# Two subtractions of a query softmax moved from GpSimd to VectorE in a fused attention and gated-MLP kernel

## The chip, the cores and the metric

The kernel runs on one core of a Trainium2 chip. A core has a matrix engine (TensorE, "PE" in the profile, with its weight loads shown apart as "PEld"), VectorE ("DVE"), ScalarE ("ACT"), GpSimd ("POOL") and SyncE ("SP", which here only issues DMAs). Each engine runs its own list of instructions in order and waits on semaphores where it needs another engine's result. The metric is the device time of one execution in microseconds; lower is better.

## The reference

Four batches of 12480 tokens with 128 channels go through an attention that passes over 49 agent tokens, and then through a two-layer MLP whose gate is x - tanh(x):

```python
def sm(a, b):
    s = scale * (a @ b.transpose(0, 2, 1))
    s = s - s.max(-1, keepdims=True)
    e = np.exp(s)
    return e / (e.sum(-1, keepdims=True) + 1e-09)
a2k = sm(agents, k)
agent_v = a2k @ v
q2a = sm(q, agents)                 # the query softmax: 12480 x 49 per batch
x = q2a @ agent_v
h = x @ w_in                        # 128 -> 2048
g = h - np.tanh(h)
out = g @ w_out                     # 2048 -> 128
```

All inputs are float32 and so is the result.

## The kernel before

Phase 1 of a batch (`phase1`) computes the agents' softmax over the keys, multiplies it with the values, and folds the result into `w_in` (`project`): what is left of the attention output and the first MLP layer is then one matmul of the query softmax `p` (49 columns per token) with a 49 x 2048 matrix. To keep float32 accuracy with the faster float32r matmuls, operands are carried as a rounded "high" part and a "low" part, the difference. `p` is kept as 98 columns (49 high, 49 low, tile `pp`), and the folded matrix as `awh` and `awl`.

The main loop walks over 100 blocks of 500 tokens (the last of each batch has 480), 25 to a batch, and over 8 steps per block, two of the 16 chunks of 2048 in each. One step is:

- TensorE: four matmuls into a two-bank PSUM tile `h` (`m1`, L538 and L539);
- ScalarE: `y = tanh(h)` (L548) and `z = y*y` (L550);
- VectorE: `g = h * z` (L553), which is the gate up to a factor for the small `h` that occur here;
- GpSimd: `gh`, the rounded high part of `g` (`high`, L582);
- VectorE: `gl = g - gh`, the low part (`low`, L587);
- TensorE: six matmuls of `gh` and `gl` with `w_out`, summed in one PSUM tile `misc` over the block's 8 steps (`m2`, L600, L601, L602). In one step of every second block `gh` and `gl` are left out and a plain float32 matmul is used instead (L598).

`gh`, `gl`, `y`, `z` and `g` have 3, 2, 2, 2 and 4 buffers; `h` has 3 PSUM buffers and `misc` 2, which the running sum shares with every smaller product.

Beside this main stream run side jobs as Python generators: the query softmax of the next pair of blocks (`q_softmax`, started once per pair, 50 in all), the transposes of `pp` (`q_transpose`, L525), and the pieces of phase 1 of the next batch. Every step of the main loop calls `next` once on each job that is under way, so a job's pieces between two `yield`s are spread over successive steps. What is recorded that way is then ordered for each engine by a scheduler, which holds to data dependencies and a few manual ones.

The query softmax of one pair works on a tile of 126 rows x 8 groups x 49. TensorE writes the scores to a `misc` tile (L494). VectorE takes the row maximum `qm` (L502). ScalarE copies the scores to SBUF as `qe` (L503), GpSimd subtracts the maximum there (L505), ScalarE takes the exponential (L507). VectorE sums (`qs`, L509), adds epsilon (L510), takes the reciprocal (L511) and scales `qe` (L512); that last one is called MUL below. ScalarE writes the rounded high half of `pp` (L515), and GpSimd writes the low half, `qe` minus that (L517).

The first softmax is stepped by hand in `fast` with `next(q0)`, between the pieces of the first batch's phase 1 (L701 to L714).

Of the kernel before, what the change touches and what calls it, by code (L numbers as in the profile page):

```python
# [12 lines left out]
F32 = mybir.dt.float32  # L13
# [6 lines left out]
ALU = mybir.AluOpType  # L20
# [4 lines left out]
A = 49  # L25
# [6 lines left out]
TT = 126  # L32
TG = 120
GT = 8
# [63 lines left out]
class Build:  # L98
# [386 lines left out]
    def q_softmax(self, halves, qt, res, TT=TT):  # L485
        nc = self.nc
        ps = self.misc()
        for t in range(GT):
            b, at, w = halves[t // BT]
            at += min(t % BT * TT, w - TT)  # L490
            for r in range(0, TT, QUART):
                m = min(QUART, TT - r)
                to = ps[r : r + m, t * A : (t + 1) * A]
                nc.tensor.matmul(to, qt[:, at + r : at + r + m], self.ag[:, b, :], start=True, stop=True)  # L494
        yield
        yield
        pv = ps[:TT, : GT * A].rearrange("p (t a) -> p t a", a=A)
        m = self.small.tile([128, GT], F32, tag="qm", name="qm")
        e = self.small.tile([128, GT, A], F32, tag="qe", name="qe")
        ev = e[:TT]  # L500
        s = self.small.tile([128, GT], F32, tag="qs", name="qs")
        nc.vector.tensor_reduce(m[:TT], pv, axis=AX.X, op=ALU.max)  # L502
        nc.scalar.copy(ev, pv)  # L503
        yield
        nc.gpsimd.tensor_tensor(ev, ev, m[:TT, :, None].broadcast_to([TT, GT, A]), ALU.subtract)  # L505
        yield
        nc.scalar.activation(ev, ev, AF.Exp, scale=SCALE)  # L507
        yield
        nc.vector.tensor_reduce(s[:TT], ev, axis=AX.X, op=ALU.add)  # L509
        nc.vector.tensor_scalar(s[:TT], s[:TT], EPS, None, ALU.add)  # L510
        nc.vector.reciprocal(s[:TT], s[:TT])  # L511
        nc.vector.tensor_tensor(ev, ev, s[:TT, :, None].broadcast_to([TT, GT, A]), ALU.mult)  # L512
        yield
        pp = self.small.tile([128, GT, A2], F32R, tag="pp", name="pp")
        nc.scalar.copy(pp[:TT, :, :A], ev)  # L515
        yield
        nc.gpsimd.tensor_tensor(pp[:TT, :, A:], ev, pp[:TT, :, :A].bitcast(F32), ALU.subtract)  # L517
        res.append(pp)

    def q_transpose(self, pp, half, res, w, TT=TT):  # L520
# [117 lines left out]
    def fast(self):  # L638
        nc, tc = self.nc, self.tc
# [4 lines left out]
        qt, pp, pT = {}, {}, {}  # L644

        def q_src(p):
            at = column(2 * p)
            return self.qT[:, at : at + width(2 * p) + width(2 * p + 1)]
# [11 lines left out]
        with ExitStack() as first:  # L660
            self.begin(first, "first")
            p1 = self.phase1(0)
            raws = [None] * 8

            def load_raw(c):
                raws[c] = self.raw_w_in(c) if c < 4 else self.raw_w_out(c - 4)

            self.wf = self.keep.tile([128, FF], F32R, tag="awh", name="awh", bufs=2).bitcast(F32)
            loads = []
            for g in range(NG):  # L670
                if g % 2 == 0 and 0 < g < 10:
                    loads.append((load_raw, g // 2 - 1))
                loads.append((self.k0, g))
            q1_load = lambda p: qt.update({p: self.q_load(q_src(p))})
            loads.append((q1_load, 0))
            for g in range(NG):
                loads.append((self.v0, g))
            loads += [(load_raw, 4), (q1_load, 1)] + [(load_raw, c) for c in (5, 6, 7)]
            free = K0

            def load(more):
                nonlocal free
                free += more
                while loads and (free > 0 or loads[0][0] not in (self.k0, self.v0)):
                    f, g = loads.pop(0)
                    free -= f in (self.k0, self.v0)
                    f(g)

            load(0)
            for g in range(NG):  # L690
                run(p1[g])
                load(1)
                if g % 2 == 1 and 2 < g < 11:
                    self.load_w_in((g - 3) // 2, raws[(g - 3) // 2])
            at = self.count() - 1
            run(p1[NG])
            run(p1[NG + 1])
            q0 = q_job(0)
            av = p1[NG + 3 : 2 * NG + 3]
            for g in range(NG):  # L700
                if g == Q0:  # L701
                    next(q0)
                    next(q0)
                    next(q0)
                next(av[g])
                next(av[g])
            next(q0)
            next(q0)
            for g in range(NV):
                next(av[g])  # L710
                load(1)
            for g in range(5):
                run(av[g])
            run(q0)  # L714
            run(t_job(0))
            run(t_job(1))
            for g in range(NV, NG):
                next(av[g])
                load(1)
            for g in range(5, NG):  # L720
                run(av[g])
# [185 lines left out]
```

## Time and profile before

| | |
|---|---|
| time, median of 3 runs | 2141.66 us (2140.11 to 2143.02) |
| the profiled execution's own time | 2142.99 us |
| its span, first to last instruction | 2141.2 us |
| mean granted TensorE clock | 0.996 |
| busy: PE / PEld / DVE / ACT / POOL | 98% / 77% / 93% / 85% / 61% |

The profile records one execution. It gives each engine's busy time, groups of instructions by source line and shape with their count and mean duration, the idle time of the engine ahead of each group with the instruction that ended it, and a timeline. In a group's row `gl<-g,gh` names the tile that is written and those that are read, and what stands after it is the shape out and in. An instruction's recorded duration overlaps that of the next one on its engine a little: VectorE starts a new instruction about 0.08 us before the record of the one ahead ends, and matmul records overlap by more.

### The profile page before, as it was taken

The numbers are of one execution on the slowest core, as the hardware profiler recorded it, in microseconds if no ns is written. First come the engines' busy times: TensorE is split into PE (matmuls) and PEld (weight loads), VectorE is DVE, ScalarE is ACT, GpSimd is POOL, SyncE is SP. The second block draws the span as 40 slices with busy tenths as digits, with TensorE's granted clock in tenths as the row PEclk, the third lists the DMA queues.
The fourth block names the chain that finished last, engine by engine and source line by source line (L and its number), as shares of the span: only waits on it lengthen the run. The fifth ranks groups of instructions, "written<-read, shape, count | busy, mean of one in ns | idle before, by whom it ended". The sixth has DMA issues, their size and how long they took to land.

```text
span 2141.2 us, 35133 instructions
## 1 busy us (share of the span) xinstructions
PE 2107.2 (98%) x13259; PEld 1658.2 (77%) x13259; DVE 1996.0 (93%) x2031; ACT 1820.5 (85%) x2136; POOL 1303.9 (61%) x858
## 2 busy tenths in 40 slices
PE   8999999999999999999999999999999999999998
PEld 7577778777777777777787777777777777778776
DVE  7899999889999998889999999988999999999998
ACT  3888888888888888888898888888888989899897
POOL 0366666556665556556576566655666767767666
PEclk9999999999999999999999999999999999999999
DMA  9312112110112111211001110111000000100000
GB/s 343 105 60 68 53 37 72 51 55 24 39 49 67 54 50 50 59 61 49 20 28 61 59 42 30 50 59 42 30 30 21 29 30 20 33 26 20 30 10 21
DMA packets 65345, 109.01 MB, mean 51 GB/s; under 512 B 3984, under 2 KB 44176, under 8 KB 65168
## 3 DMA queue, kind: packets, MB, share of 16 engines
q1 hardware_dynamic: 65168, 106.68, 15.2%
q8 instruction: 108, 1.77, 0.4%
q14 instruction: 69, 0.57, 0.1%
HBM read 81.10 MB, written 25.56 MB: 50 GB/s over the span
## 4 chain that ended last, share of the span: by engine, by line
PE 66%; DVE 18%; issue 6%; POOL 5%; ACT 4%; DMA 0%; POOLq 0%; SPq 0%; DVEq 0%; ACTq 0%
PE misc L602 12%; PE h L538 11%; PE misc L600 11%; PE h L539 11%; PE misc L601 10%; DVE g L553 9%; DVE gl L587 6%; POOL gh L582 4%; PE misc L598 3%; ACT y L548 2%; PE misc L340 2%; PE misc L494 2%; ACT z L550 1%; PE misc L279 1%; PE h L250 1%
## 5 line engine op out<-in xcount | busy, mean ns | idle before, releaser
L582 POOL TENSOR_SCALAR gh<-g 128x1000 fp32r<-128x1000 f32 (+1 forms) x743 | 1197.8, 1612 | 690.2 <-DVE g L553 387.5
L587 DVE TENSOR_TENSOR gl<-g,gh 128x1000 fp32r<-128x1000 f32 (+1 forms) x743 | 956.5, 1287 | 85.6 <-PE misc L602 42.9
L553 DVE TENSOR_TENSOR g<-h,z 128x1000 f32<-128x1000 f32 (+1 forms) x800 | 945.4, 1188 | 30.8 <-ACT z L550 28.8
L548 ACT ACTIVATE y<-h 128x1000 f32<-128x1000 f32 (+1 forms) x800 | 801.4, 1004 | 198.4 <-PE h L539 192.0
L550 ACT ACTIVATE z<-y 128x1000 f32<-128x1000 f32 (+1 forms) x800 | 823.1, 1041 | 29.2 <-DVE g L553 12.9
L538 PE MATMUL h<-pT,awh 98*128 98x500 f32 (+1 forms) x1600 | 662.5, 414 | 0.3
L539 PE MATMUL h<-pT,awl 98*128 98x500 f32 (+1 forms) x1600 | 622.0, 389 | 0.0
L602 PE MATMUL misc<-gl,wo_h 128*128 128x500 f32 (+1 forms) x1486 | 594.4, 400 | 8.2 <-DVE gl L587 7.9
L600 PE MATMUL misc<-gh,wo_l 128*128 128x500 f32 (+1 forms) x1486 | 581.7, 391 | 7.6 <-POOL gh L582 6.7
L601 PE MATMUL misc<-gh,wo_h 128*128 128x500 f32 (+1 forms) x1486 | 578.2, 389 | 0.0
L538 PEld LDWEIGHTS h<-pT,awh 98*128 98x128 f32 x1600 | 301.2, 188 | 79.8 <-issue 17.7
L539 PEld LDWEIGHTS h<-pT,awl 98*128 98x128 f32 x1600 | 303.3, 190 | 68.9 <-issue 14.5
L602 PEld LDWEIGHTS misc<-gl,wo_h 128*128 128x128 f32 x1486 | 279.0, 188 | 83.3 <-DVE gl L587 23.1
L600 PEld LDWEIGHTS misc<-gh,wo_l 128*128 128x128 f32 x1486 | 280.6, 189 | 75.3 <-POOL gh L582 21.6
L601 PEld LDWEIGHTS misc<-gh,wo_h 128*128 128x128 f32 x1486 | 279.7, 188 | 53.6
L505 POOL TENSOR_TENSOR qe<-qe,qm 126x392 f32<-126x392 f32 x50 | 46.9, 938 | 77.2 <-ACT qe L503 77.2
L517 POOL TENSOR_TENSOR pp<-qe,pp 126x392 fp32r<-126x392 f32 x50 | 55.6, 1113 | 59.6 <-ACT pp L515 59.5
L598 PE MATMUL misc<-g,wo_f 128*128 128x500 f32 (+1 forms) x196 | 90.0, 581 | 0.0
L758 ACT ACTIVATE o<-misc 128x500 f32<-128x500 f32 (+1 forms) x100 | 58.0, 580 | 16.2 <-PE misc L602 9.0
L530 ACT CAST pT<-misc 98x500 fp32r<-98x500 f32 (+1 forms) x100 | 56.7, 568 | 5.3 <-PE misc L525 4.4
L598 PEld LDWEIGHTS misc<-g,wo_f 128*128 128x128 f32 x196 | 36.9, 188 | 26.2 <-issue 22.5
L525 PEld LDWEIGHTS misc<-identr,pp 126*98 126x98 f32 x400 | 38.9, 127 | 18.4 <-POOL pp L517 6.5
(111 smaller groups left out, 853.7 us busy)
## 6 DMA issues: line engine op xcount, KB each, us to landing
kt<-kT SPq DMA_DIRECT2D x48, 512.0 KB, 3.7
qt<-qT SPq DMA_DIRECT2D x46, 500.0 KB, 3.5
outT<-o SPq DMA_DIRECT2D x46, 500.0 KB, 2.6
v<-v SPq DMA_DIRECT2D x36, 512.0 KB, 4.1
vt<-v SPq DMA_DIRECT2D x12, 512.0 KB, 5.8
raw<-w_in SPq DMA_DIRECT2D x4, 512.0 KB, 9.2
v<-w_out SPq DMA_DIRECT2D x4, 512.0 KB, 8.1
qt<-qT SPq DMA_DIRECT2D x4, 490.0 KB, 3.5
```

The costliest lines, as they stand in the source:

```text
L538: nc.tensor.matmul(h[:, c, :w], aw[0][:A2, sl], pT[:A2, :w], start=True, stop=False)
L539: nc.tensor.matmul(h[:, c, :w], aw[1][:A2, sl], pT[:A2, :w], start=False, stop=True)
L548: nc.scalar.activation(self.pair(y), h, AF.Tanh, scale=TSC)
L550: nc.scalar.activation(z, y, AF.Square)
L553: nc.vector.tensor_tensor(self.pair(g), h, self.pair(z), ALU.mult)
L582: self.nc.gpsimd.tensor_scalar(gh, g, 1.0, 0.0, ALU.mult, ALU.add)
L587: self.nc.vector.tensor_tensor(gl, g, gh.bitcast(F32), ALU.subtract)
L598: nc.tensor.matmul(acc[:, :w], wf[:, c * C : (c + 1) * C], gh[:, x], start=first, stop=last)
L600: nc.tensor.matmul(acc[:, :w], self.wo_l[:, f, :], gh[:, x], start=first, stop=False)
L601: nc.tensor.matmul(acc[:, :w], self.wo_h[:, f, :], gh[:, x], start=False, stop=False)
L602: nc.tensor.matmul(acc[:, :w], self.wo_h[:, f, :], gl[:, x], start=False, stop=last)
L758: nc.scalar.activation(o[:, at : at + w], acc[n][:, :w], AF.Copy, scale=GSC)
```

## The change

The GpSimd subtraction of the maximum (L505) and the ScalarE copy ahead of it (L503) go. One VectorE instruction takes their place, and reads the scores straight from PSUM. The GpSimd subtraction that makes the low half of `pp` (L517) becomes the same instruction on VectorE. The softmax job has one `yield` less, so what follows the subtraction comes one step of the main loop earlier in the recorded program, and one `next(q0)` in `fast` goes.

```diff
         nc.vector.tensor_reduce(m[:TT], pv, axis=AX.X, op=ALU.max)
-        nc.scalar.copy(ev, pv)
-        yield
-        nc.gpsimd.tensor_tensor(ev, ev, m[:TT, :, None].broadcast_to([TT, GT, A]), ALU.subtract)
+        nc.vector.tensor_tensor(ev, pv, m[:TT, :, None].broadcast_to([TT, GT, A]), ALU.subtract)
         yield
         nc.scalar.activation(ev, ev, AF.Exp, scale=SCALE)
         yield
...
         nc.scalar.copy(pp[:TT, :, :A], ev)
         yield
-        nc.gpsimd.tensor_tensor(pp[:TT, :, A:], ev, pp[:TT, :, :A].bitcast(F32), ALU.subtract)
+        nc.vector.tensor_tensor(pp[:TT, :, A:], ev, pp[:TT, :, :A].bitcast(F32), ALU.subtract)
         res.append(pp)
...
                 next(av[g])
                 next(av[g])
             next(q0)
-            next(q0)
             for g in range(NV):
                 next(av[g])
```

After the change GpSimd runs `gh` and nothing else in the main loop. Lines behind the edits move up by two (L553 becomes L551, L587 becomes L585, L512 becomes L510) and, in `fast`, by three.

The order below is VectorE's, in a pair of blocks of the last batch, from the row maximum of one softmax to the second `gl` behind it. Before, with buffer numbers:

```order
L502 TENSOR_REDUCE qm_19540<-misc_19481 126x8
L587 TENSOR_TENSOR gl_19553<-g_19523,gh_19525 128x1000
L587 TENSOR_TENSOR gl_19575<-g_19549,gh_19551 128x1000
L553 TENSOR_TENSOR g_19571<-h_19561,z_19569 128x1000
L553 TENSOR_TENSOR g_19593<-h_19583,z_19591 128x1000
```

The same place after the change:

```order
L502 TENSOR_REDUCE qm_19495<-misc_19436 126x8
L585 TENSOR_TENSOR gl_19508<-g_19478,gh_19480 128x1000
L503 TENSOR_TENSOR qe_19496<-misc_19436,qm_19495 126x392
L585 TENSOR_TENSOR gl_19530<-g_19504,gh_19506 128x1000
L551 TENSOR_TENSOR g_19526<-h_19516,z_19524 128x1000
L551 TENSOR_TENSOR g_19551<-h_19538,z_19549 128x1000
```

The new subtraction, L503, stands between two `gl` that followed each other before. The second place is some steps further on in the same pair, on VectorE again, from the reciprocal to the `g` behind the low half of `pp`. Before:

```order
L511 RECIPROCAL qs_19542<-qs_19542 126x8
L512 TENSOR_TENSOR qe_19541<-qe_19541,qs_19542 126x392
L553 TENSOR_TENSOR g_19637<-h_19626,z_19635 128x1000
L587 TENSOR_TENSOR gl_19641<-g_19616,gh_19618 128x1000
L553 TENSOR_TENSOR g_19657<-h_19645,z_19655 128x1000
L587 TENSOR_TENSOR gl_19661<-g_19637,gh_19639 128x1000
L553 TENSOR_TENSOR g_19679<-h_19670,z_19677 128x1000
```

After the change:

```order
L509 RECIPROCAL qs_19497<-qs_19497 126x8
L585 TENSOR_TENSOR gl_19596<-g_19572,gh_19574 128x1000
L510 TENSOR_TENSOR qe_19496<-qe_19496,qs_19497 126x392
L551 TENSOR_TENSOR g_19611<-h_19600,z_19609 128x1000
L585 TENSOR_TENSOR gl_19615<-g_19592,gh_19594 128x1000
L515 TENSOR_TENSOR pp_19566<-qe_19496,pp_19566 126x8x49
L551 TENSOR_TENSOR g_19633<-h_19624,z_19631 128x1000
```

The scaling of `qe` (MUL, now L510) stood behind the reciprocal and now stands right behind a `gl`; the new low half of `pp` (L515) stands right behind the next `gl`, with a `g` behind it. Counted over the 50 pairs of the whole program: MUL has a `gl` right ahead of it in 1 pair before and in 20 after; the low half of `pp` has a `gl` ahead in 34 pairs, and in 22 of these a `g` behind it, in 12 another `gl`; the new subtraction has a `gl` on both sides in 43. The order of the matmuls on TensorE stays as it is in the last batch but for the first transposes of each pair, which come one step later; in the other batches the small products of phase 1 also shift by a step here and there. On ScalarE the copy is gone, and around the scaling of `qe` two steps that stood as `tanh`, `tanh`, square, square now stand as `tanh`, square, `tanh`, square.

## Prediction

> **What bounds the kernel now.** I read the page's first part, then busy time by stretches, then the groups of VectorE and GpSimd, then one pair of blocks in the timeline.
>
> ```profile
> span 2141.2 us, 35133 instructions
> PE 2107.2 (98%) x13259; PEld 1658.2 (77%) x13259; DVE 1996.0 (93%) x2031; ACT 1820.5 (85%) x2136; POOL 1303.9 (61%) x858
> ```
>
> TensorE and VectorE are both nearly full, so the whole program's shares don't say which one ends last. Stretches do. The first three below are those in which phase 1 adds most to TensorE, the next four the rest of the first three batches' work, then the steady part of the last batch, and then one pair of that part.
>
> ```profile
> core 0: us, PE busy (x) PEld busy (x) DVE busy (x) ACT busy (x) POOL busy (x), PEclk, DMA share, GB/s
> 321.20:481.80 160.60, 160.60 (x1078) 127.39 (x1077) 142.16 (x147) 140.07 (x168) 95.26 (x64) 1.00 0.20 60
> 803.00:963.50 160.50, 159.66 (x1027) 126.32 (x1026) 140.79 (x144) 139.94 (x167) 95.79 (x64) 1.00 0.19 57
> 1391.80:1552.40 160.60, 160.60 (x1021) 127.71 (x1020) 141.98 (x146) 140.11 (x167) 94.64 (x63) 1.00 0.14 43
> 107.10:321.20 214.10, 212.39 (x1368) 166.44 (x1368) 205.90 (x207) 183.42 (x213) 133.55 (x88) 1.00 0.17 54
> 481.80:803.00 321.20, 318.35 (x2005) 248.81 (x2004) 308.42 (x307) 275.16 (x318) 196.41 (x130) 1.00 0.15 47
> 963.50:1391.80 428.30, 423.92 (x2684) 332.06 (x2683) 407.44 (x406) 366.91 (x428) 266.64 (x175) 1.00 0.13 42
> 1552.40:1654.90 102.50, 101.48 (x620) 79.25 (x619) 98.52 (x102) 89.93 (x105) 66.93 (x44) 1.00 0.08 26
> 1654.90:2044.90 390.00, 387.54 (x2295) 307.03 (x2294) 378.06 (x360) 344.68 (x389) 270.23 (x170) 1.00 0.08 26
> 1873.18:1912.19 39.01, 38.77 (x231) 30.85 (x230) 37.84 (x37) 34.67 (x39) 27.28 (x17) 1.00 0.08 27
> ```
>
> In the first three, VectorE idles 18.4, 19.7 and 18.6 us, about 5 us for each of the eleven pairs in them, and TensorE has no gap to speak of: TensorE sets the pace. In the next four VectorE idles 8.2 + 12.8 + 20.9 + 4.0 = 45.9 us in 1066 us, some 25 pairs, or 1.8 us a pair. In the last batch it idles 1.17 us in a pair of 39.01 us. There the two engines are abreast, and who waits changes within a pair. TensorE, where it waits:
>
> ```profile
> 1902.48 0.39 PE L538 MATMUL h<-pT,awh 98*128 98x500 f32 x1
> 1902.70 0.38 PE L539 MATMUL h<-pT,awl 98*128 98x500 f32 x1
> 1903.27 0.50 PE L600 MATMUL misc<-gh,wo_l 128*128 128x500 f32 x1 [0.18 <-POOL gh L582]
> ```
>
> Matmuls follow each other by 0.22 us; here one comes 0.57 us behind the last, 0.35 late, because `gh` came late, and `gh` follows VectorE's `g`. The 0.38 us records overlap, so PE's 98% hides gaps up to 0.16 us and says little by itself; that VectorE idles in the first three stretches says more.
>
> **What each added and removed operation costs.** The groups of VectorE, then of GpSimd:
>
> ```profile
> L587 DVE TENSOR_TENSOR gl<-g,gh 128x1000 fp32r<-128x1000 f32 (+1 forms) x743 | 956.5, 1287 | 85.6 <-PE misc L602 42.9 <-POOL gh L582 37.6 <-POOL qe L505 1.5
> L553 DVE TENSOR_TENSOR g<-h,z 128x1000 f32<-128x1000 f32 (+1 forms) x800 | 945.4, 1188 | 30.8 <-ACT z L550 28.8
> L512 DVE TENSOR_TENSOR qe<-qe,qs 126x392 f32<-126x392 f32 x50 | 29.5, 589 | 0.7
> L502 DVE TENSOR_REDUCE qm<-misc 126x8 f32<-126x392 f32 x50 | 27.8, 556 | 0.2 <-PE misc L494 0.2
> ```
>
> ```profile
> L582 POOL TENSOR_SCALAR gh<-g 128x1000 fp32r<-128x1000 f32 (+1 forms) x743 | 1197.8, 1612 | 690.2 <-DVE g L553 387.5 <-DVE qs L511 111.2 <-PE misc L601 73.3
> L517 POOL TENSOR_TENSOR pp<-qe,pp 126x392 fp32r<-126x392 f32 x50 | 55.6, 1113 | 59.6 <-ACT pp L515 59.5
> L505 POOL TENSOR_TENSOR qe<-qe,qm 126x392 f32<-126x392 f32 x50 | 46.9, 938 | 77.2 <-ACT qe L503 77.2
> ```
>
> A subtraction of this size takes GpSimd 0.94 and 1.11 us, and VectorE 0.59 (L512 has the same shape). The Trainium skill, "GPSIMD Engine Reference", section Engine selection, says the same in general: elementwise work on two inputs belongs on VectorE, about twice as fast. That sentence speaks for the change; what it leaves out is in the next rows. `gl` and `g` have the same size, yet `gl` takes 1287 ns in the mean against 1188. The difference comes from GpSimd. The steady rhythm, VectorE first:
>
> ```profile
> 1890.05 1.19 DVE L587 TENSOR_TENSOR gl<-g,gh 128x1000 fp32r<-128x1000 f32 x1
> 1891.16 1.19 DVE L553 TENSOR_TENSOR g<-h,z 128x1000 f32<-128x1000 f32 x1
> ```
>
> ```profile
> 1890.31 1.83 POOL L582 TENSOR_SCALAR gh<-g 128x1000 fp32r<-128x1000 f32 x1 [0.40 <-PE misc L601]
> ```
>
> `gl` begins first and takes its 1.19; `gh`, begun 0.26 later, takes 1.83 and ends 0.90 behind `gl`. `g`, which reads PSUM, runs beside `gh` unhurt. Where GpSimd begins first it is the other way round; both places of the softmax in this pair:
>
> ```profile
> 1873.18 0.56 DVE L502 TENSOR_REDUCE qm<-misc 126x8 f32<-126x392 f32 x1
> 1873.65 1.87 DVE L587 TENSOR_TENSOR gl<-g,gh 128x1000 fp32r<-128x1000 f32 x1
> 1875.96 1.48 DVE L587 TENSOR_TENSOR gl<-g,gh 128x1000 fp32r<-128x1000 f32 x1 [0.43 <-PE misc L602]
> ```
>
> ```profile
> 1873.44 1.03 POOL L582 TENSOR_SCALAR gh<-g 128x1000 fp32r<-128x1000 f32 x1 [0.40 <-DVE g L553]
> 1875.54 0.84 POOL L505 TENSOR_TENSOR qe<-qe,qm 126x392 f32<-126x392 f32 x1 [1.06 <-ACT qe L503]
> ```
>
> ```profile
> 1883.82 1.20 DVE L553 TENSOR_TENSOR g<-h,z 128x1000 f32<-128x1000 f32 x1 [0.70 <-ACT z L550]
> ...
> 1887.15 1.86 DVE L587 TENSOR_TENSOR gl<-g,gh 128x1000 fp32r<-128x1000 f32 x1
> ```
>
> ```profile
> 1887.00 0.96 POOL L517 TENSOR_TENSOR pp<-qe,pp 126x392 fp32r<-126x392 f32 x1
> ```
>
> Each of these three `gl` ends 1.05 or 1.06 us after GpSimd's instruction does (1874.47, 1876.38 and 1887.96): it has waited for it, and then run in full. And a small VectorE operation on two SBUF inputs fares the same when it stands right behind a `gl`, which happens once before:
>
> ```profile
> 1141.16 1.14 DVE L587 TENSOR_TENSOR gl<-g,gh 128x1000 fp32r<-128x1000 f32 x1
> 1142.23 1.38 DVE L512 TENSOR_TENSOR qe<-qe,qs 126x392 f32<-126x392 f32 x1
> ```
>
> ```profile
> 1141.32 1.88 POOL L582 TENSOR_SCALAR gh<-g 128x1000 fp32r<-128x1000 f32 x1 [1.30 <-DVE qs L511]
> ```
>
> `gh`, slowed by `gl`, ends at 1143.20, and MUL (L512) 0.41 later.
>
> Now the sum for a pair of the last batch. VectorE occupies its engine for a record's length less 0.08 us.
>
> 1. The new subtraction of the maximum: the trace has none, but L502 reads the same tile in 0.56, and L512 writes it in as much, so 0.48 of the engine. It reads only `qm` from SBUF beside PSUM, as `g` does with `z`, so I give it no wait. ScalarE's copy (L503) goes; ScalarE is not what anyone here waits for at that place. +0.48. At best it is free, because it stands where the second `gl` waited 0.43 for a buffer.
> 2. The low half of `pp`: 0.48 if undisturbed, and 1.30 behind a `gl` (1142.23 and its 1.38). The order has it there. +1.30.
> 3. MUL moves behind a `gl` too, with a `gh` under way: 1.30 in place of 0.48. +0.82.
> 4. GpSimd's two subtractions no longer hold up `gl`: 1.48 and 1.86 become 1.19. -0.29 and -0.67. The 1.87 behind the row maximum stays, since that one is `gh`'s doing.
>
> Together +1.64 us of VectorE in a pair that has 1.17 idle: the pair can't be shorter than 37.84 + 1.64 = 39.48, 0.47 more than now. The idle time is two waits, 0.43 and 0.70. If only the first is used up (the new subtraction lies in it), the pair grows by 1.64 - 0.43 = 1.21. I take 0.5, near the lower end, because the 0.70 is a wait for the square of a step whose ScalarE instructions the new order puts 1 us earlier (square ahead of the next `tanh`). The last batch and the end have 12 such pairs: +6 us, from 0 to 14.
>
> The 25 pairs of the four mixed stretches have 1.8 us idle each against at most 1.64 added, and in 12 of the program's pairs another `gl` stands behind the low half, which would have waited for `gh` anyway. Not all idle time lies at the right place. I take +0.2 us a pair, +5 in all; the ends are -0.3 (only the gains of point 4 count) and +0.8 (half the idle time can't be used), -8 to +20. The 11 pairs of the first three stretches: 0, hidden by 5 us of idle VectorE; if that cover were gone they would cost 0.5 each. The first two softmaxes lie in the opening, where VectorE works alone on much: 2 x 0.48 for each at most, I take +1 in all.
>
> Sum: 6 + 5 + 1 = +12 us on the profiled execution's 2142.99, so 2155. That execution is 1.33 above the median of the runs, 2141.66; on the median the forecast is 2154.
>
> **The rivals.**
>
> *Faster: GpSimd was the disturber, and goes.* If the low half and MUL are not held up by `gh` (because `gh` now begins elsewhere against them), point 2 is 0.48 and point 3 nothing, the subtraction hides in the 0.43 wait, and a pair of the last batch takes 0.48 + 0.05 - 0.96 = 0.43 less on VectorE. TensorE, with its 0.35 wait above, can give that back. 12 x 0.4 + 25 x 0.3 = 12 less: 2130. For it speaks that `gh` begins earlier with nothing queued ahead of it; against it that the one row with this order (1142.23) shows the wait in full. It decides if the low half's mean is under 0.7 us. The section Engine selection above is the sentence that would have it so.
>
> *No change: TensorE hides it.* VectorE's idle time takes it all: 45.9 us in the mixed stretches, and the last batch recovers through the 0.70 wait. 2142 plus or minus 4. For it: PE at 98%. Against it: 37.84 + 1.64 is more than a pair has.
>
> *Much slower: the idle time is of no use.* The order is fixed, so VectorE's waits stay where they are and 1.2 us come on each of 36 pairs, or half of that: +22 to +43, 2164 to 2185. It decides if VectorE's idle time after is as large as before. The Trainium skill, "Trainium Kernel Development and Optimization", section Performance Expectations, calls matmul busy time a bad measure of how near a kernel is to its limit and names the weight loads' share as a good one. By that sentence TensorE stands at 77% and VectorE at 93% is the bound throughout, in the first three stretches too, and the sum would be 50 x 1.2 = 60 us, or 2202. The trace agrees with it only outside those three stretches, where VectorE has no 5 us to spare.
>
> **How the numbers follow.** The forecast, slower by 5 to 30 us, has 0.50; much slower beyond that 0.10; no change 0.22; faster 0.18. A difference of 0.2%, 4.3 us, is about what a measurement here can tell from none. Faster by more than that: 0.18; within it: 0.22; slower: 0.60. For 8 in 10 the range starts at 2135, which leaves out the better half of the faster case, and ends at 2176: 2142 + 14 + 20, the upper ends of the two main terms.
>
> **What the profile after would show.** The low half on VectorE: a mean of 1.0 to 1.2 us over the 50 (34 at 1.38, 16 at 0.56); 0.56 would make point 2 wrong. MUL: a mean near 0.9 (20 of 50 at 1.38). The new subtraction: 0.55 to 0.6 without spread. GpSimd busy near 1200 (1304 less the 102 of L505 and L517). VectorE busy up by 24 + 52 + 16 = 92 us (points 1 and 2 over 50 pairs, point 3 over 20) less at most 50 x 0.96 = 48 (point 4, if each pair has both collisions): 2040 to 2088. `gl`: the mean falls by up to 48 / 743 = 65 ns, to 1222 at the lowest. A pair of the last batch: 39.3 to 40.2 us. If VectorE is up by less than 20 us, or a pair of the last batch is under 39.0, the forecast is wrong.

## The result and the profile after

| | before | after |
|---|---|---|
| time, median (lowest to highest) | 2142.11 us (4 runs) | 2159.79 us (2158.44 to 2162.3, 4 runs) |
| the profiled execution's own time | 2142.99 us | 2158.44 us |
| its span | 2141.2 us | 2156.4 us |
| mean granted TensorE clock | 0.996 | 0.998 |

The change makes the kernel slower: after / before is 1.0085, with a 95% interval of 1.0068 to 1.0103. That is 17.7 us by the medians, and 15.5 us between the two profiled executions, of which the changed kernel's is the fastest of its four. The forecast was 12 us. The first part of the page of the changed kernel:

```profile
span 2156.4 us, 35086 instructions
PE 2108.7 (98%) x13259; PEld 1654.2 (77%) x13259; DVE 2062.1 (96%) x2131; ACT 1808.4 (84%) x2086; POOL 1188.0 (55%) x758
```

GpSimd works 115.9 us less and VectorE 66.1 us more. TensorE's share is 98% as before, and again doesn't tell where time is lost. Busy time by stretches, in the changed kernel (columns as in the prediction: length, then busy time of PE, PEld, DVE, ACT and POOL): the first and the third of the stretches with most of phase 1, the steady part of the last batch, and one pair of it.

```profile
321.20:481.80 160.60, 160.38 (x1074) 126.78 (x1073) 146.92 (x155) 137.58 (x163) 81.91 (x56) 1.00 0.20 60
1391.80:1552.40 160.60, 160.39 (x1017) 126.87 (x1016) 148.06 (x158) 137.84 (x163) 83.98 (x56) 1.00 0.14 43
1654.90:2044.90 390.00, 382.41 (x2268) 301.59 (x2267) 386.27 (x371) 340.15 (x372) 248.60 (x149) 1.00 0.08 26
1884.07:1923.87 39.80, 39.02 (x232) 30.82 (x231) 39.38 (x40) 34.78 (x38) 25.04 (x15) 1.00 0.08 26
```

In the first two VectorE still idles 13.7 and 12.5 us, and TensorE has no gap: nothing is lost there. In the last batch VectorE idles 0.42 us of a pair that takes 39.80 where it took 39.01, and TensorE, 387.54 us busy before in the same 390, is down to 382.41. The bound there is now VectorE. The groups of VectorE and GpSimd:

```profile
L551 DVE TENSOR_TENSOR g<-h,z 128x1000 f32<-128x1000 f32 (+1 forms) x800 | 945.3, 1188 | 19.3 <-ACT z L548 17.8
L585 DVE TENSOR_TENSOR gl<-g,gh 128x1000 fp32r<-128x1000 f32 (+1 forms) x743 | 937.3, 1263 | 51.1 <-POOL gh L580 36.4 <-PE misc L600 11.4 <-issue 0.3
L515 DVE TENSOR_TENSOR pp<-qe,pp 126x392 fp32r<-126x392 f32 x50 | 55.1, 1102 | 0.6 <-ACT pp L513 0.6
L510 DVE TENSOR_TENSOR qe<-qe,qs 126x392 f32<-126x392 f32 x50 | 48.0, 959 | 0.1
L503 DVE TENSOR_TENSOR qe<-misc,qm 126x392 f32<-126x392 f32 x50 | 27.8, 556 | 0.1
```

```profile
L580 POOL TENSOR_SCALAR gh<-g 128x1000 fp32r<-128x1000 f32 (+1 forms) x743 | 1179.3, 1587 | 874.7 <-DVE g L551 483.2 <-PE misc L599 117.1 <-PE misc L600 94.2
```

Three instructions of the same size, three prices: the new subtraction, which reads PSUM, 556 ns and always that; MUL 959 and the low half 1102, which both read two SBUF tiles. Their means are mixtures: of the 50 low halves 17 take 0.56 us and 33 take 1.38, of the 50 MULs 24 take 0.56 and 21 1.38, with 5 between. Where it happens, on VectorE in a pair of the last batch:

```profile
1894.69 1.15 DVE L585 TENSOR_TENSOR gl<-g,gh 128x1000 fp32r<-128x1000 f32 x1
1895.76 1.39 DVE L510 TENSOR_TENSOR qe<-qe,qs 126x392 f32<-126x392 f32 x1
1897.07 1.18 DVE L551 TENSOR_TENSOR g<-h,z 128x1000 f32<-128x1000 f32 x1
1898.18 1.18 DVE L585 TENSOR_TENSOR gl<-g,gh 128x1000 fp32r<-128x1000 f32 x1
1899.29 1.38 DVE L515 TENSOR_TENSOR pp<-qe,pp 126x392 fp32r<-126x392 f32 x1
1900.59 1.19 DVE L551 TENSOR_TENSOR g<-h,z 128x1000 f32<-128x1000 f32 x1
```

and on GpSimd at the same time:

```profile
1894.82 1.91 POOL L580 TENSOR_SCALAR gh<-g 128x1000 fp32r<-128x1000 f32 x1 [0.65 <-DVE qs L509]
1898.44 1.82 POOL L580 TENSOR_SCALAR gh<-g 128x1000 fp32r<-128x1000 f32 x1 [1.70 <-PE misc L600]
```

`gh` begins just after a `gl`, is slowed by it, and ends at 1896.73 and 1900.26. MUL ends at 1897.15 and the low half at 1900.67, 0.42 and 0.41 later: each has waited some 0.82 us with nothing in the record's idle column to show for it. The `g` behind the low half comes late by that, and TensorE waits for it; its matmuls in the same pair:

```profile
1900.99 0.42 PE L523 MATMUL misc<-identr,pp 126*98 126x126 f32 x4
1901.83 0.49 PE L536 MATMUL h<-pT,awh 98*128 98x500 f32 x1 [0.42 <-DVE g L551]
...
1914.17 0.39 PE L537 MATMUL h<-pT,awl 98*128 98x500 f32 x1
1914.92 0.49 PE L598 MATMUL misc<-gh,wo_l 128*128 128x500 f32 x1 [0.36 <-POOL gh L580]
```

The first wait is new; by the starts of the matmuls around it, against their usual spacing, it costs 0.84 us, 0.42 of it idle and the rest in slower matmuls on both sides of the gap. The second was there before, 0.35 late, and is now 0.53. A delay of 0.27 ahead of the transposes, which this pair had before, is gone. That makes 0.84 + 0.18 - 0.27 = 0.75, the 0.8 us that the pair is longer. TensorE's waits over the whole program, after:

```profile
PE misc L598 <- POOL gh L580: 10.1, 25, 0.8
PE h L536 <- DVE g L551: 6.5, 16, 0.5
```

The second row had no counterpart before. From one row maximum to the next, pair by pair against before: +0.8 us by the third pair (the opening), +6.3 over the rest of the first three batches, between -0.2 and +0.1 a pair in the middle of each of the first three stretches, then 0.75 a pair, +8.0, to the end.

### The profile page after: what moved, and what is told of

It reads as the page before. It is cut to its first block, busy times and chain, and to the rows that moved or that the text cites. A ratio compares the mean times of both kernels' runs of the same rounds, so it can differ in the third digit from the quotient of the medians.

```text
span 2156.4 us, 35086 instructions
## 1 busy us (share of the span) xinstructions
PE 2108.7 (98%) x13259; PEld 1654.2 (77%) x13259; DVE 2062.1 (96%) x2131; ACT 1808.4 (84%) x2086; POOL 1188.0 (55%) x758
## 4 chain that ended last, share of the span: by engine, by line
PE 71%; DVE 17%; issue 6%; POOL 4%; ACT 1%; DMA 0%; POOLq 0%; SPq 0%; DVEq 0%; ACTq 0%
PE misc L600 13%; PE h L536 13%; PE h L537 12%; PE misc L598 12%; PE misc L599 12%; DVE g L551 7%; DVE gl L585 6%; POOL gh L580 4%; PE misc L596 3%; PE misc L340 2%; PE misc L494 2%; PE misc L279 1%; DVE pp L515 1%; PE h L250 1%; DVE qe L510 1%
## 5 line engine op out<-in xcount | busy, mean ns | idle before, releaser
L580 POOL TENSOR_SCALAR gh<-g 128x1000 fp32r<-128x1000 f32 (+1 forms) x743 | 1179.3, 1587 | 874.7 <-DVE g L551 483.2
L585 DVE TENSOR_TENSOR gl<-g,gh 128x1000 fp32r<-128x1000 f32 (+1 forms) x743 | 937.3, 1263 | 51.1 <-POOL gh L580 36.4
L551 DVE TENSOR_TENSOR g<-h,z 128x1000 f32<-128x1000 f32 (+1 forms) x800 | 945.3, 1188 | 19.3 <-ACT z L548 17.8
L548 ACT ACTIVATE z<-y 128x1000 f32<-128x1000 f32 (+1 forms) x800 | 826.4, 1040 | 30.3 <-DVE g L551 14.4
L515 DVE TENSOR_TENSOR pp<-qe,pp 126x392 fp32r<-126x392 f32 x50 | 55.1, 1102 | 0.6 <-ACT pp L513 0.6
L494 PEld LDWEIGHTS misc<-ag,qt 128*32 128x32 f32 (+1 forms) x3200 | 38.4, 109 | 18.0 <-ACT y L546 9.6
L523 PEld LDWEIGHTS misc<-identr,pp 126*98 126x98 f32 x400 | 39.7, 127 | 15.2 <-DVE pp L515 1.0
```

Source lines behind the costliest of these rows:

```text
L548: nc.scalar.activation(z, y, AF.Square)
L551: nc.vector.tensor_tensor(self.pair(g), h, self.pair(z), ALU.mult)
L580: self.nc.gpsimd.tensor_scalar(gh, g, 1.0, 0.0, ALU.mult, ALU.add)
L585: self.nc.vector.tensor_tensor(gl, g, gh.bitcast(F32), ALU.subtract)
```

## The experiments

Two theories stood against each other. W (wait): what costs is that an instruction of VectorE with two SBUF inputs, put behind a `gl`, waits for the `gh` that GpSimd has begun, or, if it begins first, makes the `gl` behind it wait: about 0.8 us either way. C (count): VectorE has 100 more instructions and is the bound outside the first three stretches; how they wait does not matter. All ratios are against the kernel before, measured on the same chip in the same session (medians 2141.1 to 2141.7 us). "A pair" is a pair of the last batch, from one row maximum to the next, in the mean of its steady part: 39.03 us before, 39.77 after. Code cuts are set against the changed kernel; `...` marks lines left out.

### One half of the change at a time

`e1_sub_only` leaves the low half on GpSimd:

```diff
-        nc.vector.tensor_tensor(pp[:TT, :, A:], ev, pp[:TT, :, :A].bitcast(F32), ALU.subtract)
+        nc.gpsimd.tensor_tensor(pp[:TT, :, A:], ev, pp[:TT, :, :A].bitcast(F32), ALU.subtract)
```

> Only the subtraction of the maximum is on VectorE (straight from PSUM, ScalarE's copy gone); the low half of p stays on GpSimd. Theory W (a VectorE instruction with two SBUF inputs waits for the GpSimd gh that is under way): the subtraction reads PSUM and takes 0.56 us without spread; it lies in a wait of gl, so it is free. What costs is the scaling of qe, which the order still puts behind a gl in 17 of 50 pairs: 17 x 0.82 = 14 us of VectorE, its mean 0.84. The 1.48 of gl beside GpSimd's subtraction goes. Time 2142 to 2148, +3 us; VectorE busy about 2025. Theory C (what counts is 0.48 us more of VectorE for each moved instruction, wherever it stands): half of the loss of 17.7 us, so 2151.

2140.51 us (11 runs), ratio 0.9995 [0.9986, 1.0004]; a pair takes 38.9. VectorE's groups in it:

```profile
L585 DVE TENSOR_TENSOR gl<-g,gh 128x1000 fp32r<-128x1000 f32 (+1 forms) x743 | 937.1, 1262 | 79.5 <-POOL gh L580 41.0 <-PE misc L600 35.6 <-issue 0.3
L510 DVE TENSOR_TENSOR qe<-qe,qs 126x392 f32<-126x392 f32 x50 | 46.4, 928 | 0.2
```

The subtraction is free; both theories had expected some loss. MUL waits for `gh` here almost as often as in the changed kernel (928 ns against 959), and that is free too: its wait alone is covered.

`e2_low_only` keeps the copy and GpSimd's subtraction of the maximum, with their `yield` and the `next(q0)` in `fast` (not shown here), and moves the low half alone:

```diff
-        nc.vector.tensor_tensor(ev, pv, m[:TT, :, None].broadcast_to([TT, GT, A]), ALU.subtract)
+        nc.scalar.copy(ev, pv)
+        yield
+        nc.gpsimd.tensor_tensor(ev, ev, m[:TT, :, None].broadcast_to([TT, GT, A]), ALU.subtract)
```

> Only the low half of p is on VectorE; copy and subtraction of the maximum as before. The order has the scaling of qe behind a gl in 1 pair and the low half behind a gl in 13, and in 28 pairs a gl right behind the low half. Theory W: low half 13 x 1.38 and 37 x 0.56, mean 0.77 us; scaling 0.59 as before; of the gl behind the low half two thirds or so wait for gh, 0.76 us each, +15 to +20 us; GpSimd's low half gone, -14. VectorE busy 2030 to 2040, time +6 to +10, 2148 to 2152. Theory C: half of the loss, 2151, with a mean of gl that does not rise.

2148.0 us (7 runs), ratio 1.0029 [1.0018, 1.004]; a pair takes 39.65. VectorE's low half, and one place of it with the `gl` behind it and GpSimd's `gh`:

```profile
L517 DVE TENSOR_TENSOR pp<-qe,pp 126x392 fp32r<-126x392 f32 x50 | 35.6, 711 | 0.6 <-ACT pp L515 0.6
```

```profile
1888.94 0.56 DVE L517 TENSOR_TENSOR pp<-qe,pp 126x392 fp32r<-126x392 f32 x1
1889.42 2.02 DVE L587 TENSOR_TENSOR gl<-g,gh 128x1000 fp32r<-128x1000 f32 x1
```

```profile
1889.21 1.18 POOL L582 TENSOR_SCALAR gh<-g 128x1000 fp32r<-128x1000 f32 x1 [0.40 <-PE misc L601]
```

The low half goes through in 0.56, but `gh` starts beside it, ahead of the next `gl`, and that `gl` takes 2.02. The wait has moved from the small instruction to the large one. Alone the two halves cost -1.0 and +6.5 us, together +17.7: they don't add. That speaks against C as a plain sum, and for a cover that the first wait uses up.

### Moving the softmax by a step

`e3_qs4` and `e5_qs2` are the changed kernel with the next pair's softmax started one step of the main loop later or earlier, so that MUL and the low half meet other neighbours:

```diff
-QS = 3
+QS = 4
```

> The changed kernel with the softmax started one step later in each pair (QS 3 to 4), so that the order puts the scaling of qe behind a g again (1 pair behind a gl instead of 20), while the low half stays behind a gl in 32. The work of each engine is the same. Theory W: scaling back to a mean of 0.58 to 0.62 us, VectorE busy down by 10 to 16 us from 2062, low half as in the changed kernel (1.05 to 1.1), time 6 to 10 us below the changed kernel, 2150 to 2154. Theory C: as the changed kernel, 2160 within 3.

2166.61 us (4 runs), ratio 1.0114 [1.0099, 1.0129]; a pair takes 40.1. MUL and the low half in it:

```profile
L515 DVE TENSOR_TENSOR pp<-qe,pp 126x392 fp32r<-126x392 f32 x50 | 48.4, 969 | 1.5 <-ACT pp L513 1.5
L510 DVE TENSOR_TENSOR qe<-qe,qs 126x392 f32<-126x392 f32 x50 | 32.4, 649 | 0.3
```

W's forecast was missed. MUL's own wait is nearly gone, as intended, but 25 `gl` now stand behind a MUL and wait for `gh`, 20.8 us in all. A pair still has two waits of 0.82 us, and VectorE idles 0.7 us in it in place of 0.4; why the kernel is slower still than the changed one was not found out.

```diff
-QS = 3
+QS = 2
```

> The changed kernel with the softmax started one step earlier (QS 3 to 2). The order puts the scaling behind a gl in 7 pairs instead of 20 and the low half behind a gl in 8 instead of 34, but in 36 pairs a gl follows right behind the low half instead of 24. Theory W: low half mean 0.65 to 0.75 us, scaling 0.65 to 0.75; against that 20 or so more gl wait for gh, +15 us; VectorE busy 2040 to 2050, time 2150 to 2157, a part of the loss back. Theory C: 2160 within 3.

2160.34 us (5 runs), ratio 1.0084 [1.007, 1.0098]; a pair takes 39.7. The three groups in it:

```profile
L585 DVE TENSOR_TENSOR gl<-g,gh 128x1000 fp32r<-128x1000 f32 (+1 forms) x743 | 976.8, 1315 | 46.2 <-POOL gh L580 31.1 <-PE misc L600 8.8 <-PE misc L330 1.8
L510 DVE TENSOR_TENSOR qe<-qe,qs 126x392 f32<-126x392 f32 x50 | 32.8, 656 | 0.4
L515 DVE TENSOR_TENSOR pp<-qe,pp 126x392 fp32r<-126x392 f32 x50 | 29.6, 592 | 0.6 <-ACT pp L513 0.6
```

Both small instructions are all but free of waits, and `gl` has risen from 1263 to 1315 ns: 39 us, the same that MUL and the low half lost (15 + 25 us). The time is the changed kernel's. That is what C forecast; W had forecast 2150 to 2157 and counted too few waits: 35 `gl` now wait behind the low half, and 29 behind the new subtraction, where the changed kernel has 11 and 4. Whoever stands next to `gh` pays.

`e6_sub_qs4` is the same step later for the subtraction alone:

```diff
-QS = 3
+QS = 4
...
-        nc.vector.tensor_tensor(pp[:TT, :, A:], ev, pp[:TT, :, :A].bitcast(F32), ALU.subtract)
+        nc.gpsimd.tensor_tensor(pp[:TT, :, A:], ev, pp[:TT, :, :A].bitcast(F32), ALU.subtract)
```

> Only the subtraction of the maximum moved, with the softmax started one step later in each pair (QS 4). The scaling then stands behind a g, and in 25 pairs a gl right behind it, which by theory W waits instead: VectorE no better off than with QS 3, time 2138 to 2146. If the place of the scaling were what decides, it would be faster than the kernel with only that subtraction moved (2140.5), 2134 to 2138.

2143.17 us (11 runs), ratio 1.0008 [0.9999, 1.0017]: without the low half on VectorE the step costs 2.7 us against `e1_sub_only`, with the low half 6.8 against the changed kernel, so the later start by itself does not explain `e3_qs4`.

### The wait taken away

By W, a wait for `gh` can be taken away by giving the instruction one SBUF input. `e8_psum_last` does it in the 11 pairs whose softmax runs in the last batch: the reciprocal and the scaled `p` stay in the scores' PSUM tile, so MUL and the low half read one tile from PSUM and one from SBUF. Engines and count of the instructions are the changed kernel's; `psum` is true in these pairs alone.

```diff
+        sp = ps[:TT, GT * A : GT * A + GT] if psum else s[:TT]
+        pe = pv if psum else ev
-        nc.vector.reciprocal(s[:TT], s[:TT])
-        nc.vector.tensor_tensor(ev, ev, s[:TT, :, None].broadcast_to([TT, GT, A]), ALU.mult)
+        nc.vector.reciprocal(sp, s[:TT])
+        nc.vector.tensor_tensor(pe, ev, sp[:TT, :, None].broadcast_to([TT, GT, A]), ALU.mult)
...
-        nc.scalar.copy(pp[:TT, :, :A], ev)
+        nc.scalar.copy(pp[:TT, :, :A], pe)
...
-        nc.vector.tensor_tensor(pp[:TT, :, A:], ev, pp[:TT, :, :A].bitcast(F32), ALU.subtract)
+        nc.vector.tensor_tensor(pp[:TT, :, A:], pe, pp[:TT, :, :A].bitcast(F32), ALU.subtract)
```

> The changed kernel, but in the last batch's eleven pairs the reciprocal and the scaled p stay in the scores' PSUM tile, so that the scaling and the low half each have one input from SBUF and one from PSUM. Same instructions, same lengths. Theory W: both take 0.56 us there, a pair of the last batch 38.9 to 39.3 in place of 39.8, time 6 to 10 us below the changed kernel, 2150 to 2154; the batches before unchanged. Theory C: a pair stays at 39.8, 2160. A third possibility: the scores' PSUM buffer is now held some 10 us longer, and the running sum of the next block waits for it; then a pair is above 39.8.

2151.28 us (4 runs), ratio 1.005 [1.0034, 1.0065], 8.5 us less than the changed kernel; a pair takes 38.90. All 22 instructions concerned take 0.56 us. Up to the last batch the kernel loses what the changed kernel loses (+7.7 us at its start, there +7.2). Its row for the last batch, to set beside that of the changed kernel above:

```profile
1654.90:2044.90 390.00, 386.70 (x2303) 308.32 (x2302) 380.53 (x381) 343.33 (x381) 244.98 (x150) 1.00 0.08 26
```

This looks clear, but the order was not quite the same: the scheduler had exchanged, once in each pair, a `gl` and the `g` ahead of it behind the low half (`gl`, `gl`, `g`, `g` in place of `gl`, `g`, `gl`, `g`), a square and a `tanh` on ScalarE, and two groups of matmuls. `e12_psum_order` is the same kernel with manual dependencies that hold all engines to exactly the changed kernel's order, as its trace shows on each. The cut shows them alone, without the lines that find the places:

```diff
+            if self.after_low in (1, 2):
+                new = list(self.nc.cur_bb.bb.instructions)[at2:]
+                if self.after_low == 1:
+                    y = next(k for k in new if k.engine == ET.Activation)
+                    self.tc.add_manual_dep(y, zs, info, reason="order")
+                else:
+                    g, gl = [k for k in new if k.engine == ET.DVE]
+                    self.tc.add_manual_dep(gl, g.name, info, reason="order")
...
+                k = next(k for k in list(self.nc.cur_bb.bb.instructions)[at4:] if k.engine == ET.PE)
+                self.tc.add_manual_dep(k, self.first_gh, info, reason="order")
```

> The PSUM variant of the last batch once more, but with every engine's instructions held in exactly the changed kernel's order. In the PSUM variant before, one gl and one g behind the low half stood exchanged on VectorE, and likewise a square and a tanh on ScalarE and two groups of matmuls on TensorE, so its 8.5 us could come from the order. Theory W (the waits for gh cost): MUL and the low half take 0.56 us in all 11 pairs, a pair of the last batch takes 38.9 to 39.2 us, the time is 2150 to 2155 us. If the order did it (O): a pair stays at 39.6 to 39.8 us and the time at 2158 to 2161 us, though both instructions take 0.56.

2145.43 us (10 runs), ratio 1.0019 [1.0009, 1.0028]: 14.4 us less than the changed kernel, more than W expected, and a pair takes 38.44, 0.6 us less than before the change. VectorE and GpSimd at the two places:

```profile
1889.55 1.18 DVE L590 TENSOR_TENSOR gl<-g,gh 128x1000 fp32r<-128x1000 f32 x1
1890.64 0.56 DVE L513 TENSOR_TENSOR misc<-qe,misc 126x392 f32<-126x392 f32 x1
1891.11 1.19 DVE L556 TENSOR_TENSOR g<-h,z 128x1000 f32<-128x1000 f32 x1
1892.22 1.19 DVE L590 TENSOR_TENSOR gl<-g,gh 128x1000 fp32r<-128x1000 f32 x1
1893.33 0.56 DVE L518 TENSOR_TENSOR pp<-misc,pp 126x392 fp32r<-126x392 f32 x1
1893.80 1.19 DVE L556 TENSOR_TENSOR g<-h,z 128x1000 f32<-128x1000 f32 x1
```

```profile
1889.68 1.94 POOL L585 TENSOR_SCALAR gh<-g 128x1000 fp32r<-128x1000 f32 x1 [0.65 <-DVE misc L512]
1892.48 1.82 POOL L585 TENSOR_SCALAR gh<-g 128x1000 fp32r<-128x1000 f32 x1 [0.87 <-PE h L542]
```

`gh` is under way as in the changed kernel, and both instructions run in 0.56 beside it. The last batch:

```profile
1654.90:2044.90 390.00, 389.18 (x2317) 312.01 (x2316) 383.15 (x386) 346.55 (x386) 252.47 (x152) 1.00 0.08 26
```

TensorE has nearly no gap. C falls: kind, order and count of the instructions are the changed kernel's, and without the two waits, 0.82 us each, a pair is 1.3 us shorter. Of the rest only ScalarE's copy of the high half differs a little, which reads PSUM and takes 0.48 us in place of 0.52. The exchanges in `e8_psum_last` had cost a third of that, 0.46 us a pair. At the start of the last batch this kernel stands at +8.7 us, at its last softmax at +2.4; PSUM in the other batches was not tried.

The Trainium skill, "GPSIMD Engine Reference", section Key points, says that GpSimd shares its SBUF interfaces with VectorE and that the contention is with VectorE instructions "in a 2-port perf mode or with two SBUF inputs". The trace agrees: of one size, the instructions with two SBUF inputs take 0.56 or 1.38 us, those with one input from PSUM always 0.56.

`e7_low_reduce` goes the other way to one SBUF input: a maximum over the high half in the place of the low half, while ScalarE fills the other 48 low columns.

```diff
-        nc.vector.tensor_tensor(pp[:TT, :, A:], ev, pp[:TT, :, :A].bitcast(F32), ALU.subtract)
+        nc.scalar.copy(pp[:TT, :, A + 1 :], ev[:, :, 1:])
+        nc.vector.tensor_reduce(pp[:TT, :, A], pp[:TT, :, :A].bitcast(F32), axis=AX.X, op=ALU.max)
```

> The same, with a VectorE instruction of the low half's length in its place that has one SBUF input: a maximum over the high half of p, written into one of the low columns, with ScalarE writing the rest (this changes what is computed). The transposes wait for it as they did for the low half. Theory W: it takes 0.55 us with no spread and gl behind it waits no more than elsewhere; a pair of the last batch 39.0 to 39.3, time 2139 to 2147, at most 6 us above the kernel without it. Theory C: a VectorE instruction is a VectorE instruction: 2156 to 2162, a pair at 39.8, as the changed kernel.

2155.52 us (4 runs), ratio 1.0065 [1.005, 1.008]; a pair takes 39.7. The instruction itself:

```profile
L516 DVE TENSOR_REDUCE pp<-pp 126x8 fp32r<-126x392 f32 x50 | 27.6, 551 | 0.6 <-ACT pp L513 0.6
```

551 ns without spread, as W has it, but hardly any time came back: the time is just under C's range, and far from W's. Two things are mixed into this run beside the low half: the extra ScalarE copy, and the exchange of `gl` and `g` behind the low half, which the scheduler made here too in every steady pair of the last batch. There VectorE's and GpSimd's order is that of `e8_psum_last`, and the pair is 0.8 us longer than in that kernel; MUL, which waits in this one (1.38 us in place of 0.56), accounts for as much.

### The same place, loaded from ScalarE

`e4_low_scalar` takes the low half off VectorE and has ScalarE write the low columns with a second copy:

```diff
-        nc.vector.tensor_tensor(pp[:TT, :, A:], ev, pp[:TT, :, :A].bitcast(F32), ALU.subtract)
+        nc.scalar.copy(pp[:TT, :, A:], ev)
```

> The changed kernel without the low half's subtraction on any engine: ScalarE writes a second copy of p there instead (this changes what is computed). It gives the price of the low half on VectorE as a whole. Theory W, as the first four runs have it (a small instruction on two SBUF inputs costs about 1.3 us of VectorE between two steps, because either it or the gl behind it waits for gh): a pair of the last batch back to 38.9 to 39.0 us, as where only the subtraction of the maximum was moved, time 2136 to 2143. Theory C (0.48 us of VectorE and no more): a pair near 39.3, 2147 to 2151.

2156.01 us (4 runs), ratio 1.0071 [1.0055, 1.0086]; a pair takes 39.7. Both theories missed this one. `gl` in it:

```profile
L585 DVE TENSOR_TENSOR gl<-g,gh 128x1000 fp32r<-128x1000 f32 (+1 forms) x743 | 926.6, 1247 | 102.5 <-POOL gh L580 78.7 <-PE misc L600 18.5
```

VectorE, busy only 2002.0 us, now idles for `gh` instead of working: 78.7 us against 36.4. The square of the same step stands behind the extra copy, `g` behind the square, `gh` behind `g`. This suggests a theory S: at this place of the pair the chain square, `g`, `gh`, `gl` is so tight that half a microsecond of ScalarE, too, lengthens the pair. `e9_scalar_extra` tests it on the kernel that costs nothing, `e1_sub_only`, by writing the high half twice:

```diff
         nc.scalar.copy(pp[:TT, :, :A], ev)
+        nc.scalar.copy(pp[:TT, :, :A], ev)
         yield
-        nc.vector.tensor_tensor(pp[:TT, :, A:], ev, pp[:TT, :, :A].bitcast(F32), ALU.subtract)
+        nc.gpsimd.tensor_tensor(pp[:TT, :, A:], ev, pp[:TT, :, :A].bitcast(F32), ALU.subtract)
```

> Only the subtraction of the maximum moved (low half on GpSimd), and ScalarE writes the high half of p twice, 0.51 us more of ScalarE at that place. The two runs in which ScalarE wrote the low half came out at 2156 although VectorE had less to do. If ScalarE's extra copy is why (theory S: at this place of the pair no engine of the chain has room), this one is slow too, 2150 to 2157, a pair of the last batch 39.3 to 39.7. If it was the order of VectorE there, 2139 to 2145 and a pair at 38.9 to 39.0.

2158.72 us (4 runs), ratio 1.0082 [1.0064, 1.01]. Fifty more copies of 0.52 us, and 18.2 us more than `e1_sub_only`, a little above what S expected. But this does not show S, since the order changed with the copy. From the 41st softmax on, three lengths take turns (39.8 us in the mean), though each pair has the copy: 38.5 us where `gl` and `g` alternate behind MUL as in `e1_sub_only`, 40.2 to 40.3 where the scheduler exchanged two of them once, and 40.7 where it did so twice. One such place, in a pair of 40.26:

```profile
1824.44 1.18 DVE L586 TENSOR_TENSOR gl<-g,gh 128x1000 fp32r<-128x1000 f32 x1
1826.56 1.20 DVE L586 TENSOR_TENSOR gl<-g,gh 128x1000 fp32r<-128x1000 f32 x1 [0.94 <-POOL gh L581]
1827.68 2.30 DVE L552 TENSOR_TENSOR g<-h,z 128x1000 f32<-128x1000 f32 x2
```

The second `gl` waits 0.94 us for its `gh`. In `e4_low_scalar`, which has the same exchange, it waits 0.92 or 0.93 in every pair of the last batch. A pair with the copy and without the exchange is no longer than one of `e1_sub_only` (38.9). What the copy costs in an unchanged order was not tried. Whatever it is, it does not replace W: in `e12_psum_order` ScalarE's instructions are those of the changed kernel, and 0.48 us of VectorE fit at this place, where 1.30 did not.

### What the low half costs in all

`e10_no_low` leaves the low half out; its columns are zero from the start:

```diff
-        pp = self.small.tile([128, GT, A2], F32R, tag="pp", name="pp")
+        pp = self.ppz[self.turn % 2]
+        self.turn += 1
...
-        nc.vector.tensor_tensor(pp[:TT, :, A:], ev, pp[:TT, :, :A].bitcast(F32), ALU.subtract)
```

> The changed kernel with no low half at all: two fixed buffers hold p, their low columns are zero from the start (this leaves part of the accuracy out). No extra work on ScalarE this time. The price of the low half on VectorE in whole: theory W (0.48 us of work and 0.82 us of wait) says a pair of the last batch at 38.9 to 39.0 and 2136 to 2142, some 19 us below the changed kernel; if the low half's 0.48 us of work were all, 2150.

2131.16 us (5 runs), ratio 0.9958 [0.9943, 0.9972], below what was expected; a pair takes 38.45. The last batch in it:

```profile
1654.90:2044.90 390.00, 390.00 (x2326) 313.83 (x2325) 381.06 (x376) 347.90 (x386) 262.25 (x153) 1.00 0.08 26
```

TensorE has no gap left. The low half on VectorE costs 2159.79 - 2131.16 = 28.6 us, on GpSimd 2140.51 - 2131.16 = 9.4 us; both prices take in what the scheduler reordered. In a pair of the last batch it is 39.77 - 38.45 = 1.32 us on VectorE, and with neither instruction waiting (`e12_psum_order`, 38.44) nothing.

`e11_low_gp_last` gives the low half back to GpSimd in the last batch alone (`PQ` is 39, the first of its pairs):

```diff
-        nc.vector.tensor_tensor(pp[:TT, :, A:], ev, pp[:TT, :, :A].bitcast(F32), ALU.subtract)
+        (nc.gpsimd if gp else nc.vector).tensor_tensor(pp[:TT, :, A:], ev, pp[:TT, :, :A].bitcast(F32), ALU.subtract)
...
-            return self.q_softmax(halves, qt.pop(p), pp[p])
+            return self.q_softmax(halves, qt.pop(p), pp[p], gp=p >= PQ)
```

> The changed kernel with the low half back on GpSimd in the last batch's eleven pairs alone. It splits the loss: by theory W the last batch returns to 38.9 to 39.0 us a pair and the first three batches keep theirs, about 8 us, 2149 to 2153. If the last batch were slow for what happens before it, it stays at 39.8 and 2160.

2150.84 us (4 runs), ratio 1.0049 [1.0031, 1.0067]; a pair takes 38.91. So 9.0 of the 17.7 us are lost in the last batch and 8.7 in the first three. That waits cause the loss is shown for the last batch; for the first three, where the same two durations stand in the trace, it is inferred. Of the kernels that compute all of the reference, none is faster than the one before; `e1_sub_only` is its equal, with less work on GpSimd. That kernel up to the last batch, and `e12_psum_order` from there on, would come out some 7 us under it, by an estimate from their traces (-0.6 at the start of the last batch, and 6.3 gained in it); it was not run.

## Why the prediction was right, and where its size was off

The direction, the place and the mechanism held; the loss was 17.7 us where 12 were forecast.

*Point 1, the new subtraction, without a wait and at best free: right.* 556 ns in the mean, no spread, and by `e1_sub_only` free. It fills the wait that the second `gl` had. The `gl` on either side of it in the changed kernel:

```profile
1884.54 1.87 DVE L585 TENSOR_TENSOR gl<-g,gh 128x1000 fp32r<-128x1000 f32 x1
1886.33 0.55 DVE L503 TENSOR_TENSOR qe<-misc,qm 126x392 f32<-126x392 f32 x1
1886.87 1.20 DVE L585 TENSOR_TENSOR gl<-g,gh 128x1000 fp32r<-128x1000 f32 x1
```

The second takes 1.20 in place of 1.48, and the first its 1.87, both as point 4 said.

*Point 2, the low half at 1.30 behind a `gl`: right.* 33 of 50 take 1.38, where 34 were counted from the order, and the mean of 1102 lies between the 1.0 and 1.2 us forecast. `e10_no_low` prices it at 1.32 in a pair. That this is so near to 1.30 is in part luck: it is a difference of two pair lengths, and in the shorter TensorE has no gap left.

*Point 3, MUL behind a `gl`: right in duration, wrong in weight.* 21 waits of 1.38 against 20 forecast, 959 ns against "near 0.9". But `e1_sub_only` has nearly the same waits and no loss. A wait costs what the cover behind it leaves; MUL's finds cover enough when the low half isn't there too. With both waits taken away the pair falls to 38.44, so the two together cost 1.3 us of it. Whether the low half's wait alone would fit, without MUL's, was not tried in this order; nearest is `e2_low_only`, where MUL takes 0.57, one `gl` waits 0.83 behind the low half, and a pair takes 39.65.

*Point 4, `gl` freed of GpSimd's subtractions: right where the pair of the last batch was read, too large over the program.* The mean falls by 24 ns, not the 65 at most: counted over the trace, the some 28 us lost beside those subtractions are gone, but 12 `gl` right behind a MUL and 11 right behind a low half now lose 10.0 and 9.1 us to `gh`, where before 5 behind a MUL lost 4.1.

*The sum.* The floor of 39.48 us a pair held. The term that was mis-sized is 0.5 for each pair of the last batch: it measured 0.75. It was taken near the lower end because the earlier square was to make up for the 0.70 wait of `g`; in the pair that wait for the square is 0.42 us long still, and TensorE has a new wait for `g`. The 12 pairs were to lose 6 us, and lost 8 in the profile and 9 by `e11_low_gp_last`. The 25 mixed pairs were put at 0.2 each, 5 us; they measured 6.3 in the profile, and 7.9 by the experiments (8.7 less the opening), so 0.25 to 0.32 each. How that divides between MUL and the low half, pair by pair, stays open. The opening, +1, measured 0.8, and the 11 pairs hidden by TensorE lost nothing.

*The rivals.* "Faster" was to decide if the low half's mean lay under 0.7 us; it is 1.10. The sentence that went with it, in the Trainium skill, "GPSIMD Engine Reference", section Engine selection, is near the truth for a single instruction here (0.56 us on VectorE where it doesn't wait, 0.96 on GpSimd at 1887.00, 1.7 times as long) and not true of the kernel: the same subtraction costs 28.6 us on VectorE and 9.4 on GpSimd. "No change" needed VectorE's idle time to take all of it; it takes MUL's wait alone (`e1_sub_only`), and not both. "Much slower" needed the idle time to be as large as before; it fell from 145.2 to 94.3 us. Nor did the sum of 2202 come about that went with it: in the stretch from 321 us TensorE was busy 160.38 of 160.60 us, and there 5 us of VectorE's added work cost nothing. The sentence behind that sum, in the Trainium skill, "Trainium Kernel Development and Optimization", section Performance Expectations, would have read room there from the weight loads, 126.78 us of the 160.60.

## What to carry to other kernels

Ahead of moving an elementwise operation from GpSimd to VectorE, count its SBUF inputs and look what GpSimd runs beside its new place: an instruction with two SBUF inputs may wait there as long as GpSimd's instruction lasts, or hand that wait to the next such instruction, and reading one operand from PSUM avoids both. A wait of that kind stands in no idle column; it shows as two durations of one shape, so read the spread and not the mean. Price an added half microsecond by its place in the step and not by the engine's share of busy time: here it was free at one place of VectorE's list, and came to 1.3 us a pair, its wait and MUL's included, at another. And when an edit lets a scheduler choose a new order, compare the orders before naming a cause: here an exchange of neighbours came with four of the experiments, and only in `e12_psum_order`, which held the order, could the two be told apart.

## What the runs showed of the hardware that was not expected

- Who starts first goes first, in whole instructions, and either side pays when it comes second. `gh` takes 1.03 us when it begins first (1884.34 in the changed kernel, which held up the `gl` at 1884.54 to 1.87) and 1.82 begun 0.26 us behind a `gl`. Shifting the small instruction by a step (`e5_qs2`) moved 39 us of waiting from it to `gl` and changed the total time by no more than the measurement can tell.
- Where VectorE's instruction reads one tile from PSUM, not even a `gh` that is already held up by a `gl` touches it: 0.56 us at 1890.64 and 1893.33 in `e12_psum_order`.
- One exchange of neighbours on each of VectorE, ScalarE and TensorE (`e8_psum_last` against `e12_psum_order`) is worth 0.46 us a pair, 5.9 us by the medians, with every instruction the same.
